# A spectral mixing layer and an expert layer in one kernel: neighbouring transfers of gathered token rows, of stage-2 blocks and of x joined into single ones

## The chip, the cores and the metric

The kernel runs as one launch on one core of a Trainium2 chip. The metric is device time in microseconds (us) of that core. TensorE (PE), VectorE (DVE), ScalarE (ACT), GpSimd (POOL) and SyncE (SP) run side by side, each through its own list of instructions in order. SP, ACT and POOL also issue transfers (DMAs), which sixteen DMA engines carry out.

## The reference, cut to what matters

```python
# x (8, 2496, 256); filters (1249, 256); float32
X = np.fft.rfft(x, axis=1)
y = np.fft.irfft(X * (filt_r + 1j * filt_i), n=2496, axis=1)

x = y.reshape(19968, 256)                 # the tokens
expert = token_ids * 2654435761 % 8
for e in range(8):                        # w1 (8, 256, 1024), w2 (8, 1024, 256)
    out[expert == e] = np.maximum(x[expert == e] @ w1[e], 0) @ w2[e]
```

Each of the eight batches is filtered along its 2496 positions by way of a Fourier transform, and then each token goes through the two matrices of the one expert that its id names.

## The kernel before, in words

**Mixing.** 2496 is split as 39 x 64. The position n is 64*n1 + n2, and the 64 values of n2 are laid out as three groups (h) of 21 with one left over. A batch passes through these steps:

- `load1` brings x in blocks (v = 0, 1, 2) of eight values of n2: partition 3*n1 + h of the block holds position 64*n1 + H0[h] + j, with H0 = (42, 0, 21). It issues one transfer per h, each of 39 partitions (line 249); the batch 0 one with h = 1 is issued by ACT, all others by SP.
- `stage1` multiplies by a DFT matrix of 39 (`wf`), and ACT stores the result to DRAM (`d1`, line 297, from 120 partitions).
- `load2` reads `d1` back turned, four frequencies at a time (`SG`): partition 2*n2 + p, where p says real or imaginary part. It issues one transfer per p on SP, each of 64 partitions (line 303).
- `forward` multiplies by a second DFT and by the filters, `back` goes the first step back, and ACT stores four frequencies at a time to `d2`, again one transfer per p (line 342).
- `load4` reads `d2` (SP, line 406), `stage3` takes the last step, and POOL scatters the finished tokens into `xs` in DRAM, sorted by expert (line 433).

Batches 0 and 1 keep part of this on the chip and do without `d2` or without both.

**Experts.** The sorted tokens lie in 85 tiles of 256 rows in `xs`; a row has 256 values and the token's number (`W` = 260 words). 80 tiles are always worked through (`NSURE`), five more if they are used. `load(i)` (line 835) fetches tile i: four transfers of 64 columns each into partitions 32*q to 32*q + 31 of the tile `xg`, and one transfer of the 256 token numbers into `no`. All are issued by ACT, but for those of tile 1 and the first three of tile 0, which SP issues. `token_parts` (line 852) turns `xg` by DVE into the operand of the products. `up` makes the first product, `down` the second; from tile 50 on (`WS`) `both` makes them. `store` scatters the rows to the output from POOL by the numbers in `no`.

**Order.** It is written out by hand: a list of (time in tiles, piece of work) pairs puts the mixing of batches 2 to 7 between the tiles. The tiles fall into five stages (they begin at tiles 0, 10, 20, 30 and 50); the first tile of a stage can be fetched only when the batches of that stage have been scattered. `ask` (line 1028) decides when a tile is fetched: inside `up` or `both`, just behind the ACT copy of the first product (lines 898 and 963) and ahead of ACT's relus (lines 891 and 953); or, within a stage, one tile sooner, inside `down`. `xg` has two buffers. Behind a tile's products SP issues the weights of the tile after next (lines 464, 467 and 469), 1 MB each.

Of the kernel before, what the change touches and what calls it, by code (L numbers as in the profile page):

```python
# [11 lines left out]
F32 = mybir.dt.float32  # L12
# [7 lines left out]
P = 128  # L20
B, S, C = 8, 2496, 256
# [7 lines left out]
N1, N2 = 39, 64  # L29
NS, NQ = N1 // 2 + 1, 64  # L30
H, HN = 3, 21
H0 = (2 * HN, 0, HN)
NR = H * N1
NK = 2 * H * NS
SG = 4
XG = 4
NU = (HN + XG) // XG
XL = 2 * XG
# [4 lines left out]
TB = 256  # L43
NT = (N + E * (TB - 1)) // TB
W = C + 4
# [28 lines left out]
def dft_tables():  # L74
    n1 = np.arange(N1)
    n2 = np.array([H0[i % H] + i // H for i in range(N2)])
    s, q = np.arange(NS), np.arange(NQ)
    ph = 2 * np.pi * np.outer(n1, s) / N1
    w = np.stack([np.cos(ph), -np.sin(ph)], 1)
    wf = np.zeros((N1, H, H, 2, NS))  # L80
    wi = np.zeros((H, 2, NS, H, N1))
    v = np.stack([2 * np.cos(ph), -2 * np.sin(ph)], 0)
    v[0, :, 0], v[1, :, 0] = 1.0, 0.0
    for h in range(H):
        wf[:, h, h] = w
        wi[h, :, :, h] = v.transpose(0, 2, 1) / S

    kap = np.where(q[:, None] < 32, s + N1 * q[:, None], s + N1 * (95 - q[:, None]))  # L90
    sg = np.where(q < 32, 1.0, -1.0)[:, None]
    th = 2 * np.pi * ((n2[:, None, None] * kap) % S) / S
    c, sn = np.cos(th), np.sin(th)
    d = np.zeros((2, N2, NS, 2, NQ))
    d[0, :, :, 0] = c.transpose(0, 2, 1)
    d[1, :, :, 0] = sn.transpose(0, 2, 1)
    d[0, :, :, 1] = (-sn * sg).transpose(0, 2, 1)
    d[1, :, :, 1] = (c * sg).transpose(0, 2, 1)
    f32 = np.float32
    return (wf.reshape(NR, NK).astype(f32), wi.reshape(NK, NR).astype(f32),  # L100
            d.transpose(1, 0, 2, 3, 4).reshape(P, NS, P).astype(f32))
# [24 lines left out]
def kernel(  # L126
# [9 lines left out]
):  # L136
    nc = tc.nc
    wf_host, wi_host, d_host = dft_tables()
    wf_dram = nc.inline_tensor(wf_host, name="wf_tbl")
    wi_dram = nc.inline_tensor(wi_host, name="wi_tbl")  # L140
# [42 lines left out]
    def slot(kind):  # L183
        slots[kind].append(slots[kind].pop(0))
        return slots[kind][-1]
# [30 lines left out]

    put_off = {2: [], 3: []}

    class Batch:


# [13 lines left out]
        def load1(self, v):  # L235

            k = self.b * NV + v if self.b < 2 else NV + NV * (self.b > 2) + v
            if self.b == 2 and v == 2:
                xt = x2pool.tile([NR, XL, C], F32, name="x_2_2", tag="x")
            elif k <= NV and self.b < 2:  # L240
                xt = wts[0:NR, k, :].rearrange("p (j c) -> p j c", c=C)
            else:
                xt = xpool.tile([NR, XL, C], F32, name=f"x_{self.b}_{v}", tag="x")
            self.x[v] = xt

            n = min(XL, HN + 1 - XL * v)
            for h in range(H):

                (nc.scalar if self.b == 0 and h == 1 else nc.sync).dma_start(out=xt[h:NR:H, 0:n, :],
                                  in_=bass.AP(tensor=x.tensor, offset=x.offset + (self.b * S + H0[h] + XL * v) * C,  # L250
                                              ap=[[N2 * C, N1], [C, n], [1, C]]))

        def products(self, w, rows, cols, src, dst, copy, u, name):

# [43 lines left out]

        def load2(self, g):
            t2 = slot("t2")  # L300
            for p in range(2):
                a0 = p * NS + SG * g
                nc.sync.dma_start(out=t2[p:P:2, :, :],
                                  in_=self.d1[:, a0:a0 + SG, :])
            self.t2[g] = t2

        def forward(self, u):
# [18 lines left out]
        def back(self, u):  # L326
            if self.d2 is None:
                self.d2 = dpool.tile([N2, 2 * NS, C], F32, name=f"d2_{self.b}", tag="d2")
            pr = self.p.pop(u)
            half = SG // 2  # L330
            if u % half == 0:
                self.g = slot("g")
            ps = fps.tile([P, 2, C], F32, name=f"pc_{self.b}_{u}", tag="f")
            for i in range(2):
                nc.tensor.matmul(out=ps[:, i, :], lhsT=e_t[:, 2 * u + i, :], rhs=pr[:, i, :],  # L335
                                 start=True, stop=True)
            i0 = 2 * (u % half)
            nc.scalar.copy(out=self.g[:, i0:i0 + 2, :], in_=ps[:])  # L338
            if u % half == half - 1:
                for p in range(2):  # L340
                    a0 = p * NS + SG * (u // half)
                    nc.scalar.dma_start(out=self.d2[:, a0:a0 + SG, :],
                                        in_=self.g[p:P:2, :, :])

        def stage1_c(self, u):
            v, j0 = divmod(XG * u, XL)
# [439 lines left out]
    head += [(98 + 5 * u, lambda u=u: second.stage3(u)) for u in range(NU)]  # L788
    head += [(99 + 5 * u - 3 * (u == 5), lambda u=u: third.stage1(u)) for u in range(NU)]
    head += [(123.5, lambda: begin()), (123.6, lambda: [load(i) for i in range(2)])]  # L790
    head += [(124, lambda: [nc.sync.dma_start(out=dram, in_=chip) for dram, chip in put_off[2]])]
    head += [(125 + .1 * g, lambda g=g: third.load2(g)) for g in range(4)]
# [23 lines left out]
    for e in range(E):  # L816
        t = 34.3 + 1.5 * e
# [8 lines left out]
    xg, to_rows, parts, rows = {}, {}, {}, {}  # L826
# [8 lines left out]
    def load(i):  # L835

        g = gath.tile([P, TB // 32, C // 4], F32, name=f"xg_{i}", tag="xg")
        no = nums.tile([P, 2], I32, name=f"no_{i}", tag="no")
        rows = xs[tiles[i] * TB:(tiles[i] + 1) * TB, :]
        moves = [(g[32 * q:32 * q + 32, :, :], rows[:, 64 * q:64 * q + 64].rearrange("(a t) c -> t a c", t=32))  # L840
                 for q in range(4)]
        moves.append((no[:].bitcast(F32), rows[:, C:C + 1].rearrange("(h p) c -> p (h c)", p=P)))
        for k, (to, src) in enumerate(moves):
            ld = (nc.sync if i < 2 and (i or k < 3) else nc.scalar).dma_start(out=to, in_=src)
            for b in range(STAGES[stage_of[i]], B):
                tc.declare_no_dep(ld.ins, group=f"xs_{b}", reason="the tiles of a stage hold tokens of its batches alone")
            if stage_of[i] < G - 1:
                tc.declare_no_dep(ld.ins, group="xs_pad", reason="places without a token lie in the last stage alone")
            tc.add_to_no_dep_group("xs_read", ld.ins)
        xg[i], to_rows[i] = g, no  # L850
# [177 lines left out]
    def ask(i, sooner=False):  # L1028

        j = asked[0]  # L1030
        if j <= i + 2 or (sooner and j == i + 3 < NT and stage_of[j] == stage_of[j - 1]):
            if j < NT:
                load(j)
                asked[0] += 1
# [48 lines left out]
    def rest(k):  # L1083
        with tc.If(used[0] > blocks[k][0]):
            for i in blocks[k]:
                ht = work.tile([P, 2, FP, P], F32, name=f"ht_{i}", tag="ht")
                if i >= NSURE + 2:
                    for j in ((i, i + 1) if i == NSURE + 2 else (i + 1,)):
                        if j < NT:
                            load(j)  # L1090
                    token_parts(i)
                token_sums(i)
                weight_sums(i, nc.vector)
                up(i, ht)
                weights(i + 2, 0)
                down(i, ht)
                store(i)
                weights(i + 2, 1)
            if k + 1 < len(blocks):
                rest(k + 1)  # L1100
# [30 lines left out]
```

## Time and profile before

| | us |
|---|---|
| median of 3 runs | 1428.36 (1425.63 to 1430.61) |
| the profiled execution | 1424.24 |
| its span in the trace | 1422.5 |

| engine | busy us | share of the span |
|---|---|---|
| PE | 1373.4 | 97% |
| DVE | 890.2 | 63% |
| POOL | 830.3 | 58% |
| ACT | 416.6 | 29% |

| transfers | issued by | count, KB each |
|---|---|---|
| `xg<-xs`, line 844 | ACT, SP | 321 and 7, 64 |
| `no<-xs`, line 844 | ACT, SP | 81 and 1, 1 |
| `mid<-d` (`load2`), line 303 | SP | 70, 256 |
| `d<-mid` (`back`), line 342 | ACT | 60, 256 |
| x (`load1`), line 249 | SP, ACT | 69 and 3, 312 or 234 |

In the profile, "waits" lists say which engine sat idle before which line and what ended it. A name with q (ACTq, SPq) is the engine's sequencer, which waits and issues transfers; while ACTq waits, ACT does nothing else. "DMA share" is the mean busy share of the sixteen DMA engines, by the durations of their packets. The span of 1422.5 us falls into a head of 122 us (batches 0 and 1, routing), a turn to the tiles (122 to 150), a middle in which tiles and mixing alternate (to 1043), and 370 us of tiles alone.

### The profile page before, as it was taken

To read this page: it belongs to the slowest core of one execution; us is meant where nothing else is said; L and a number is where in the kernel's file an instruction comes from. 1 tells how busy PE (TensorE), PEld (TensorE's weight loads), DVE (VectorE), ACT (ScalarE), POOL (GpSimd) and SP (SyncE) were. 2 spreads that over 40 slices of the span, in tenths; PEclk is the share of its full clock that TensorE was granted. 3 is DMA by queue.
4 is the path that set the end of the run, shared out by engine and by line. 5 is a ranking of instruction groups with operands and counts; after the bars stand their busy time and mean duration, and the time that the engine had idled before them with its cause. 6 is when DMAs were issued, how large, how long until landed. Compare 5 with 4: busy or idle time off the path is not lost.

```text
span 1422.5 us, 26307 instructions
## 1 busy us (share of the span) xinstructions
PE 1373.4 (97%) x9398; PEld 1273.3 (90%) x9398; DVE 890.2 (63%) x1636; ACT 416.6 (29%) x760; POOL 830.3 (58%) x736
## 2 busy tenths in 40 slices
PE   7898999999999999999999999999999999999997
PEld 7776888989888988889999899999999999999997
DVE  7773575575556566445665477657766776676775
ACT  4554122223232223232222222222222222222222
POOL 6167243844665565578533587788855566555563
PEclk9999899999999999999999999999999999999999
DMA  8677765757987698888755785887742526261611
GB/s 222 206 235 216 212 218 121 260 192 245 269 270 224 183 284 264 261 262 273 241 167 131 219 258 170 235 242 235 254 138 68 190 62 199 46 218 42 215 46 35
DMA packets 244505, 278.33 MB, mean 196 GB/s; under 512 B 125171, under 2 KB 213670, under 8 KB 234948
## 3 DMA queue, kind: packets, MB, share of 16 engines
q1 hardware_dynamic: 95149, 179.33, 40.2%
q10 hardware_dynamic: 129303, 52.69, 15.4%
q0 software_dynamic: 19920, 44.59, 8.9%
q8 instruction: 77, 1.26, 0.4%
q14 instruction: 56, 0.46, 0.1%
HBM read 293.65 MB, written 86.15 MB: 267 GB/s over the span
## 4 chain that ended last, share of the span: by engine, by line
PE 86%; DMA 8%; DVE 3%; issue 1%; ACT 1%; ACTq 0%; SPq 0%; POOLq 0%; POOL 0%; DVEq 0%
PE dps L922 22%; PE up_b L887 9%; PE up_a L887 6%; PE up_c L887 6%; PE pd L267 5%; PE pb L312 4%; PE dnc L949 4%; PE dnb L949 4%; PE dna L949 4%; PE upc L944 4%; PE upa L944 4%; PE pc L335 3%; PE pa L267 3%; DMA t<-d 2%; PE upe L944 2%; PE upb L944 2%
## 5 line engine op out<-in xcount | busy, mean ns | idle before, releaser
L922 PE MATMUL dps<-wts,ht 128*128 128x256 f32 x1600 | 370.9, 382 | 6.1 <-ACT ht L891 6.1
L922 PEld LDWEIGHTS dps<-wts,ht 128*128 128x128 f32 x1600 | 304.7, 192 | 50.6 <-ACT ht L891 7.3
L1014 POOL DMA_INDIRECT out_dram<-osb,no x158 | 165.2, 1046 | 219.2 <-DVE osb L956 137.8
L433 POOL DMA_INDIRECT xs<-o,sidx x176 | 177.0, 1006 | 168.7 <-ACT o L269 73.3
L877 POOL TENSOR_TENSOR tw<-wts 128x512 f32<-128x512 f32 x158 | 205.1, 1298 | 116.0 <-DMA wts<-in_moe_w_dram 92.4
L877 POOL TENSOR_TENSOR tw<-wts,tw 128x512 f32<-128x512 f32 x158 | 206.1, 1305 | 6.2
L894 DVE TENSOR_TENSOR ht<-up_b,ht 128x512 f32<-128x512 f32 x150 | 103.7, 691 | 114.6 <-PE up_b L887 91.2
L891 ACT ACTIVATE ht<-ht 128x512 f32<-128x512 f32 x150 | 94.3, 630 | 188.8 <-DVE ht L894 164.9
L322 DVE TENSOR_TENSOR z<-pb,filt 64x512 f32<-64x512 f32 x160 | 110.2, 689 | 30.9 <-PE pc L335 28.9
L927 DVE COPY osb<-dps 128x512 f32<-128x512 f32 x50 | 34.6, 691 | 150.2 <-PE dps L922 149.7
L887 PE MATMUL up_a<-xt,wts 128*128 128x128 f32 x800 | 115.3, 277 | 9.1 <-DVE xt L855 4.9
L887 PEld LDWEIGHTS up_a<-xt,wts 128*128 128x128 f32 x800 | 105.9, 193 | 12.7 <-DVE xt L855 5.3
L887 PE MATMUL up_b<-st,tw 128*128 128x128 f32 x800 | 107.4, 278 | 2.7 <-DVE ht L894 1.8
L887 PEld LDWEIGHTS up_b<-st,tw 128*128 128x128 f32 x800 | 98.1, 193 | 4.9 <-issue 3.7
L953 ACT ACTIVATE ht<-ht 128x512 f32<-128x512 f32 x90 | 56.6, 630 | 122.1 <-DVE ht L956 75.8
L894 DVE TENSOR_TENSOR ht<-up_c,ht 128x512 f32<-128x512 f32 x100 | 69.0, 690 | 37.2 <-PE up_c L887 32.4
L338 ACT COPY mid<-pc 128x512 f32<-128x512 f32 x60 | 35.0, 584 | 154.8 <-PE pc L335 91.5
L267 PE MATMUL pd<-t,wi_t 120*117 120x256 f32 x320 | 77.5, 385 | 2.6 <-DMA t<-d 2.6
L318 DVE TENSOR_TENSOR y<-pb,filt 128x512 f32<-128x512 f32 x80 | 55.1, 689 | 37.8 <-PE pb L312 35.6
L269 ACT COPY o<-pd 117x512 f32<-117x512 f32 x80 | 45.0, 585 | 104.4 <-DMA xg<-xs 45.4
L312 PE MATMUL pb<-mid,d_t 128*128 128x256 f32 x280 | 74.1, 388 | 1.1 <-DVE z L322 1.1
L898 ACT COPY ht<-up_a 128x512 f32<-128x512 f32 x50 | 29.3, 587 | 150.6 <-PE up_a L887 120.7
(210 smaller groups left out, 2466.1 us busy)
## 6 DMA issues: line engine op xcount, KB each, us to landing
wts<-in_moe_w_dram SPq DMA_DIRECT2D x162, 1024.0 KB
xg<-xs ACTq DMA_DIRECT2D x321, 64.0 KB
mid<-d SPq DMA_DIRECT2D x70, 256.0 KB
d<-mid ACTq DMA_DIRECT2D x60, 256.0 KB
d_t<-t2s SPq DMA_DIRECT2D x15, 1024.0 KB
e_t<-t2s SPq DMA_DIRECT2D x15, 1024.0 KB
x<-in_x_dram SPq DMA_DIRECT2D x39, 312.0 KB
t<-d SPq DMA_DIRECT2D x12, 960.0 KB
```

Source lines behind the costliest of these rows:

```text
L267: nc.tensor.matmul(out=ps[0:cols * H, k, :], lhsT=w[:], rhs=src[:, 2 * i + k, :], start=True, stop=True)
L312: nc.tensor.matmul(out=ps[:, i, :], lhsT=d_t[:, s, :], rhs=rhs, start=True, stop=True)
L322: nc.vector.tensor_tensor(out=z[b], in0=ps[a], in1=f_t[1][64 * hi:64 * hi + 64, s1:s1 + 2, :], op=OP.mult)
L433: st = nc.gpsimd.indirect_dma_start(out=xs[:], out_offset=bass.IndirectOffsetOnAxis(ap=index, axis=0), in_=rows, in_offset=None, bounds_ch ...
L877: eng.tensor_tensor(t[k][:], p, q, op=OP.subtract)
L887: nc.tensor.matmul(out=ps[bank][:, f, :], lhsT=w[:, f * P:(f + 1) * P], rhs=xx, start=first and f == 0, stop=True, skip_group_check=True)
L891: nc.scalar.activation(out=out, in_=in_, func=AF.Relu)
L894: nc.vector.tensor_tensor(out, ps[bank][:], other, op=OP.add)
L922: nc.tensor.matmul(out=ps[:, h, :], lhsT=ht[:, h, fp, :], rhs=w2[:, fp, :], start=(fp == 0), stop=(fp == FP - 1))
L944: nc.tensor.matmul(out=ps[:, f, :], lhsT=w[:, f * P:(f + 1) * P], rhs=xx, start=first and f == 0, stop=True, skip_group_check=True)
L949: nc.tensor.matmul(out=ps[:, 0, :], lhsT=a[:, f, :], rhs=b[:, f, :], start=first and f == 0, stop=True, skip_group_check=True)
L1014: st = nc.gpsimd.indirect_dma_start(out=out[:], out_offset=bass.IndirectOffsetOnAxis(ap=to_rows[i][:, h:h + 1], axis=0), in_=o[:, h, :], i ...
```

## The change

- `load1`: the three transfers of a block become one, of 117 partitions. Partition 3*n1 + h now holds position 64*n1 + 21*h + j; the rows of `wf` are put in that order on the host. Batch 0 has no x transfer on ACT any more.
- `load2` and `back`: the two parts p go in one transfer of 128 partitions; the DRAM side is read with (n2, p) as one index.
- `load`: the four transfers of a tile become one into all 128 partitions. Partition 32*q + t now holds the rows 8*t to 8*t + 7 of the tile, and the numbers in `no` are fetched in the order that fits. On the DRAM side the transfer has the dimensions (4 column blocks, 256 rows, 64 values), and that of the numbers (4, 64, 1) after merging; the chip side has 128 partitions in both. SP issues the rows of tiles 0 and 1 and the numbers of tile 1, ACT all else.

No arithmetic instruction is added or removed.

```diff
@@ dft_tables
-        wf[:, h, h] = w
+        wf[:, H0[h] // HN, h] = w
@@ class Batch
+    def halves(d):
+        return d[:].rearrange("n (p s) c -> (n p) s c", p=2)
@@ load1
-            for h in range(H):
-                (nc.scalar if self.b == 0 and h == 1 else nc.sync).dma_start(out=xt[h:NR:H, 0:n, :],
-                                  in_=bass.AP(tensor=x.tensor, offset=x.offset + (self.b * S + H0[h] + XL * v) * C,
-                                              ap=[[N2 * C, N1], [C, n], [1, C]]))
+            nc.sync.dma_start(out=xt[:, 0:n, :],
+                              in_=bass.AP(tensor=x.tensor, offset=x.offset + (self.b * S + XL * v) * C,
+                                          ap=[[N2 * C, N1], [HN * C, H], [1, n * C]]))
@@ load2
-            for p in range(2):
-                a0 = p * NS + SG * g
-                nc.sync.dma_start(out=t2[p:P:2, :, :],
-                                  in_=self.d1[:, a0:a0 + SG, :])
+            nc.sync.dma_start(out=t2, in_=halves(self.d1)[:, SG * g:SG * g + SG, :])
@@ back
-                for p in range(2):
-                    a0 = p * NS + SG * (u // half)
-                    nc.scalar.dma_start(out=self.d2[:, a0:a0 + SG, :],
-                                        in_=self.g[p:P:2, :, :])
+                g0 = SG * (u // half)
+                nc.scalar.dma_start(out=halves(self.d2)[:, g0:g0 + SG, :], in_=self.g)
@@ load
-        moves = [(g[32 * q:32 * q + 32, :, :], rows[:, 64 * q:64 * q + 64].rearrange("(a t) c -> t a c", t=32))
-                 for q in range(4)]
-        moves.append((no[:].bitcast(F32), rows[:, C:C + 1].rearrange("(h p) c -> p (h c)", p=P)))
+        moves = [(g[:], bass.AP(tensor=rows.tensor, offset=rows.offset, ap=[[C // 4, 4], [W, TB], [1, C // 4]])),
+                 (no[:].bitcast(F32), bass.AP(tensor=rows.tensor, offset=rows.offset + C, ap=[[W, 4], [8 * W, 32], [4 * W, 2], [1, 1]]))]
         for k, (to, src) in enumerate(moves):
-            ld = (nc.sync if i < 2 and (i or k < 3) else nc.scalar).dma_start(out=to, in_=src)
+            ld = (nc.sync if i < 2 and (i or k < 1) else nc.scalar).dma_start(out=to, in_=src)
```

## The prediction

> **What bounds the kernel now.** The page's busy table comes first (PE 97% of the span), then the chain of waits: 86% of it is PE and 8% is DMA. So PE sets the time wherever it has work, and a change to transfers can only win what PE idles, or make PE idle more. The PE records leave 40 us without work. The list of PE's waits shares out the gaps behind the head:
>
> ```profile
> PE dps L922 <- ACT ht L891: 6.1, 2, 3.1
> PE up_a L887 <- DVE xt L855: 4.9, 1, 4.9
> PE up_a L887 <- ACT ht L898: 4.2, 3, 2.0
> PE pd L267 <- DMA t<-d: 2.6, 2, 2.0
> ```
>
> Columns: total us, times, longest. The first and third lines, 10.3 us in five gaps (at 150, 396, 499, 605 and 789 us), are PE waiting for an ACT copy or relu. The timeline shows why ACT was late:
>
> ```profile
> 780.31 0.87 ACTq L297 DMA_DIRECT2D d<-mid  x2
> 781.27 3.20 ACTq L844 DMA_DIRECT2D xg<-xs  x4
> 790.32 0.38 ACTq L844 DMA_DIRECT2D no<-xs  x1
> 790.74 0.59 ACT L898 COPY ht<-up_a 128x512 f32<-128x512 f32 x1 [10.20 <-DMA xg<-xs]
> 791.38 0.71 PE L887 MATMUL up_a<-xt,wts 128*128 128x128 f32 x4 [1.98 <-ACT ht L898]
> ```
>
> ACT issues a tile's five transfers between its own pieces of work. In the records of the semaphores, the transfers of SP and ACT take eight completion semaphores in turn, and an issue waits until the transfer that held its semaphore before has landed. Here the `no` issue stood from 784.5 to 790.2 for the store of 780.31, the copy behind it was late, and PE lost 1.98 us.
>
> Second, how full the DMA engines are. By stretches (us; then busy us and count of each engine; PE clock, DMA share, GB/s):
>
> ```profile
> 250.00:350.00 100.00, 99.54 (x598) 90.05 (x597) 61.59 (x101) 30.12 (x54) 59.02 (x53) 1.00 0.74 235
> 350.00:450.00 100.00, 97.88 (x591) 88.29 (x590) 58.87 (x100) 30.68 (x55) 59.24 (x54) 1.00 0.87 260
> 450.00:550.00 100.00, 96.78 (x570) 86.61 (x570) 58.01 (x105) 26.97 (x49) 52.47 (x48) 0.98 0.82 245
> 550.00:650.00 100.00, 97.67 (x580) 86.76 (x580) 46.96 (x80) 30.30 (x55) 67.92 (x63) 1.00 0.84 259
> 1043.00:1200.00 157.00, 156.19 (x1394) 155.62 (x1393) 112.41 (x252) 43.50 (x89) 89.61 (x75) 1.00 0.42 127
> ```
>
> In the middle the sixteen engines are over 80% busy on average; in the last 370 us under half. What counts is therefore how evenly a joined transfer lies on them.
>
> **How a transfer is split.** The page's line for ACT's queue answers this:
>
> ```profile
> q10 hardware_dynamic: 129303, 52.69, 15.4%
> ```
>
> From the issues' counts and sizes, ACT's data packets are 82,176 of 256 B (321 `xg`), 20,736 of 4 B (81 `no`), 3,840 of 4 KB (60 `d<-mid`), 14,400 of 1 KB (other `d<-mid`) and 373 others: 121,525. That leaves 7,778 for completions. 490 transfers on sixteen engines each would give 7,840, 62 too many. Of the 490, three have 39 partitions, seventeen 120 and six 40: if each runs on the largest number up to 16 that divides its rows (13, 15, 10), 9 + 17 + 36 = 62 are missing. It fits exactly. So a transfer is split into equal numbers of outer rows. In every one of these both sides have the same number of rows. The new `xg` and `no` have 128 on the chip's side and 4 on the DRAM side; no row of before has such a pair. If the smaller decides, they run on 4 engines; if the chip's side does, on 16 as now. I take 4: a split in whole outer rows of a source with 4 of them has no more pieces.
>
> (The Trainium skill, "DMA: Bandwidth & Descriptors", section "Why a DMA increments its semaphore by 16 and not by 1", has the count of engines as the largest up to 16 that divides the slowest dimension of both sides; that is 4 here. The same page's "Rules for kernel authors" says to coalesce many small transfers into one large one. By the second rule alone the sum below would keep only its first term, about 1420; by the first it keeps all of them. The trace agrees with the first where the sides are equal, and shows no unequal pair.)
>
> **The change part by part.**
>
> x and stage 2: x goes from 72 transfers to 24; 39 and 117 rows both divide by 13, so the same 8 KB packets lie on the same 13 engines. `load2` goes from 70 to 35 and `back` from 60 to 30; 64 and 128 rows both give 16 engines and the same 4 KB packets. What goes are issues of 0.87, 0.63 and 0.57 us on SP and ACT, which PE covers (97.7 of 100 us busy in 550:650). In the head the chain is transfers of the same bytes. Cost 0; bounds -1 and 0.
>
> Issues on ACT: 893 transfers in all become 534, so a semaphore comes round later, and ACT issues two per tile instead of five (0.56 us each). The 10.3 us of gaps can go. What is late next is the tile's own data, so I take **-8**; bounds -10.3 and 0.
>
> The first tile: PE waits 4.9 us at 137 for tile 0. The chain has 2.31 us from the last of four issues (138.46) to landing. The joined one is issued at 137.6, once instead of in turns, but has 256 packets on each engine instead of 64. The trace's 256-byte packets take 20.6 ns on mean: 5.3 us instead of 1.3. First completions come 1.8 us after an issue here; landing about 137.6 + 1.8 + 5.3 = 144.7 instead of 140.8: **+3.5**; bounds -1 (sixteen engines) and +4.
>
> The middle: a tile's `xg` and `no` cost 1,024 x 20.6 + 256 x 9.1 ns = 23.4 us of engine time. That is 1.5 us on each of sixteen, but 5.9 on each of four: 4.4 more per tile on those four. 45 tiles are fetched in 250:1043, one in 17.6 us, so their share rises by 0.25: to 0.99, 1.12, 1.07 and 1.09 in the four stretches shown. Every other transfer that uses all engines ends when these four end. The part above 1 is 12 + 7 + 9 = 28 us. The shares hold waiting, though: 8 KB packets take 376 ns on mean, 309 at the fastest, 1 KB ones 58 and 46; at the fastest durations the shares are 17% lower and nothing is over 1. So 0 to 28; I take half, **+14**.
>
> Turns of a batch in the middle: the chain passes through transfers that end last there:
>
> ```profile
> 366.81 13.93 DMA t<-d
> 382.19 12.91 DMA wts<-in_moe_w_dram
> ...
> 586.18 5.45 DMA d<-mid
> 591.69 11.78 DMA t<-d
> ```
>
> Each stands behind up to one tile's rows more on the four engines, 4.4 us. There are five batches with a store and a load to and from `d2`; PE loses only 2.6 us at `t<-d` now, so most is covered by the tiles between. Of 5 x 4.4 = 22 I take **+6**; bounds 0 and 22.
>
> The last 370 us: ACT issues a tile's rows just behind the copy at line 963 and must then do its relus:
>
> ```profile
> 1101.53 2.28 ACTq L844 DMA_DIRECT2D xg<-xs  x4
> 1103.85 0.50 ACTq L844 DMA_DIRECT2D no<-xs  x1
> 1104.93 0.63 ACT L953 ACTIVATE ht<-ht 128x512 f32<-128x512 f32 x1 [2.82 <-DVE ht L956]
> ```
>
> The rows are needed one step (12.4 us) later by DVE. Alone they land in 1.8 + 5.9 us; beside 2 MB of weights on the same engines (64 packets of 1 KB and 8 of 8 KB at 46 and 309 ns: 5.4 us) in about 13. So only tiles with a change of expert on them lose something: **+3**; bounds 0 and 51 (rival 2).
>
> Sum: -8 + 3.5 + 14 + 6 + 3 = +18.5 on the profiled execution's 1424.2 gives 1442.7. That execution lies 4.1 us under the median of the runs, against which mine is compared: **1447 us**.
>
> **Rivals.**
>
> 1. *Sixteen engines after all.* Then only the first term is left, with -1 at the first tile: 1428.4 - 9 = about 1419, at best 1417. For it: the chip's side has 128 rows and could decide. Against: the exact divisors above. This is also the case in which the change does what its words say.
>
> 2. *ACT held behind its own long transfer.* When the queues are full, an `xg` issue takes up to 2.4 us instead of 0.46 (144.8 to 149.7, behind three stores: three in a row at 1.4 to 1.7), and PE then lost 3.1 us. If the `no` issue has to stand until the 256 packets ahead of it have gone out, ACT is held 0.4 + 5.3 + 0.5 = 6.2 us per tile instead of 2.8. In the last stretch the second product starts at 1106.7, 5.1 us after the first issue at 1101.5, and needs a relu of 0.63 us first: held over some 4.5 us, PE waits. 1.7 us x 30 tiles = 51 on top of the sum: 1447 + 51 = about 1498. It decides from 4.5 us held.
>
> 3. *Gain and load even out:* four engines, but the shares' waiting part gives way (terms of 0 to 4 us for the middle): 1428.4 - 8 + 3.5 + 4 = 1428.
>
> **How the numbers follow.** Forecast (four engines, +6 to +45 on the median) 0.42; rival 1 0.24; rival 2 0.2; rival 3 0.14. This kernel's measurement can tell 0.3%, 4.3 us. Rival 1 is faster but for a little, rival 3 mostly within: faster 0.25, within 0.3% 0.13, slower 0.62. The range goes from rival 1 (1416) to rival 2 (1498); the forecast's own range is 1434 to 1473.
>
> **What would show it.** On four engines the packets on ACT's queue are 121,152 of data and 1,471 completions, 122,623; on sixteen 124,555. PE's waits for ACT (lines 891 and 898 before) go from 10.3 to under 3 us. DVE's wait for the first `xg` grows by 3 us. The stretches 350 to 650 lengthen, with DMA shares no higher. In the last stretch ACT is held between the `xg` issue and its relu: under 4.5 us for the forecast, over it for rival 2. A shorter middle with PE at 98% would prove me wrong.

## The result, and the profile after

The changed kernel takes 1591.49 us in the median of six runs (1587.42 to 1595.99), the kernel before 1424.41 us in six beside it. The ratio is 1.118 (95% interval 1.115 to 1.122): 12% slower, far outside the predicted range. The profiled execution took 1590.27 us, with a span of 1588.6, 166.1 more than before.

From the page of the kernel after: PE's busy time, the line of ACT's queue, and the chain by engine.

```profile
PE 1418.0 (89%) x9398; PEld 1312.0 (83%) x9398; DVE 897.5 (56%) x1636; ACT 411.4 (26%) x760; POOL 825.4 (52%) x736
...
q10 hardware_dynamic: 122623, 51.72, 12.4%
...
PE 46%; ACTq 11%; DMA 2%; DVE 2%; ACT 1%; issue 1%; POOL 0%; POOLq 0%; DVEq 0%; SPq 0%
```

The 122,623 packets are those that four engines per tile fetch give, to the packet. The completions say it too: the semaphore of an `xg` transfer takes one step at once and then exactly four. New in the chain is ACTq, ACT's sequencer, with 11% (it was 0%).

PE's list of waits (total us, times, longest):

```profile
PE up_a L881 <- ACT ht L892: 56.0, 10, 15.3
PE dne L943 <- ACT ht L947: 43.9, 8, 7.9
PE dps L916 <- ACT ht L885: 21.4, 3, 15.5
PE up_a L881 <- DVE xt L849: 8.8, 1, 8.8
```

Lines 885, 892 and 947 are ACT's relus and copy (891, 898 and 953 before); `up_a`, `dps` and `dne` are products of `up`, `down` and `both`. The waits for these three lines were 10.3 us and are 121.3. The timeline at the longest issue of all (lines in between are left out):

```profile
389.47 0.55 ACTq L838 DMA_DIRECT2D xg<-xs  x1
390.14 22.15 ACTq L838 DMA_DIRECT2D no<-xs  x1
412.39 0.58 ACT L892 COPY ht<-up_a 128x512 f32<-128x512 f32 x1 [22.90 <-issue]
413.02 1.22 PE L881 MATMUL up_a<-xt,wts 128*128 128x128 f32 x4 [15.35 <-ACT ht L892]
```

The issue of `xg` is over in 0.55 us. The issue of the numbers behind it stands for 22.15 us; it is the duration of the issue itself that is long, not a wait for a semaphore ahead of it. The copy behind it is late, and PE idles 15.35 us. Over the whole run, this kind of issue takes 518 us of ACT (81 issues, median 4.36 us); it was 41 us before (0.46).

Where the time came from, by stretches that begin and end at the same work (the middle, then the tiles alone). Before, then after:

```profile
142.00:1044.00 902.00, 883.81 (x5394) 800.81 (x5395) 539.19 (x850) 246.47 (x438) 545.44 (x478) 0.99 0.75 228
1044.00:1415.00 371.00, 369.56 (x3300) 368.60 (x3298) 261.37 (x591) 102.41 (x206) 208.03 (x173) 1.00 0.38 111
```

```profile
142.00:1148.00 1006.00, 910.17 (x5396) 822.31 (x5396) 548.88 (x851) 244.04 (x438) 542.00 (x478) 0.95 0.66 205
1148.00:1581.00 433.00, 387.99 (x3296) 386.09 (x3296) 259.43 (x591) 99.44 (x206) 207.18 (x172) 0.94 0.31 94
```

The middle is 104 us longer and the last part 62. In the middle PE is without work for 96 us instead of 18, in the last part for 45 instead of 1. The rest is PE's own busy time, 26 and 18 us more for the same instructions, at a granted clock of 0.95 and 0.94 instead of 0.99 and 1.00. The DMA engines are less busy than before.

In the last part two kinds of tiles stand side by side. One without weights in flight, and one behind 2 MB of them (lines in between are left out here too):

```profile
1167.57 0.53 ACTq L838 DMA_DIRECT2D xg<-xs  x1
1168.14 3.18 ACTq L838 DMA_DIRECT2D no<-xs  x1
1171.37 1.15 ACT L947 ACTIVATE ht<-ht 128x512 f32<-128x512 f32 x2 [3.27 <-DVE ht L950]
...
1204.13 0.40 SPq L462 DMA_DIRECT2D wts<-in_moe_w_dram  x1
1204.88 0.33 SPq L464 DMA_DIRECT2D d_t<-t2s  x1
1205.09 0.53 ACTq L838 DMA_DIRECT2D xg<-xs  x1
1205.66 10.65 ACTq L838 DMA_DIRECT2D no<-xs  x1
1217.05 2.08 PE L943 MATMUL dne<-e_t,ht 128*128 128x128 f32 x8 [6.69 <-ACT ht L947]
```

Of the 29 issues in this part 21 take 2.7 to 3.7 us, and PE does not notice; eight take 8.1 to 11.6 us, and these are the eight waits of 43.9 us in all.

### The profile page after: what moved, and what is told of

Same layout as the page of the kernel before. It is cut to its first block, busy times and chain, and to the rows that moved or that the text cites. A ratio compares the mean times of both kernels' runs of the same rounds, so it can differ in the third digit from the quotient of the medians.

```text
span 1588.6 us, 25818 instructions
## 1 busy us (share of the span) xinstructions
PE 1418.0 (89%) x9398; PEld 1312.0 (83%) x9398; DVE 897.5 (56%) x1636; ACT 411.4 (26%) x760; POOL 825.4 (52%) x736
## 3 DMA queue, kind: packets, MB, share of 16 engines
q10 hardware_dynamic: 122623, 51.72, 12.4%
## 4 chain that ended last, share of the span: by engine, by line
PE 46%; ACTq 11%; DMA 2%; DVE 2%; ACT 1%; issue 1%; POOL 0%; POOLq 0%; DVEq 0%; SPq 0%
ACTq L838 10%; PE dps L916 8%; PE up_b L881 5%; PE dnc L943 4%; PE dna L943 4%; PE dnb L943 3%; PE up_a L881 3%; PE up_c L881 3%; PE upa L938 3%; PE upc L938 2%; PE dne L943 2%; PE pc L334 1%; PE pd L269 1%; PE upe L938 1%; PE upb L938 1%; PE upg L938 1%
## 5 line engine op out<-in xcount | busy, mean ns | idle before, releaser
L881 PE MATMUL up_a<-xt,wts 128*128 128x128 f32 x800 | 123.6, 290 | 64.8 <-ACT ht L892 56.0
L881 PEld LDWEIGHTS up_a<-xt,wts 128*128 128x128 f32 x800 | 113.0, 204 | 70.2 <-ACT ht L892 58.3
L881 PE MATMUL up_b<-st,tw 128*128 128x128 f32 x800 | 114.2, 289 | 1.9 <-DVE ht L888 1.4
L881 PEld LDWEIGHTS up_b<-st,tw 128*128 128x128 f32 x800 | 104.8, 204 | 3.7 <-issue 3.4
L199 DVE TENSOR_TENSOR filt<-ht 128x512 f32<-128x512 f32 x60 | 42.3, 705 | 73.7 <-ACT ht L947 73.7
```

The lines of the kernel that those rows point to most:

```text
L881: nc.tensor.matmul(out=ps[bank][:, f, :], lhsT=w[:, f * P:(f + 1) * P], rhs=xx, start=first and f == 0, stop=True, skip_group_check=True)
```

## The experiments

Each kernel ran beside runs of the kernel before on the same chip; the chips differ (the kernel before takes 1453 us on those of the first eight, 1428 us on that of the last two), so ratios to it are given. The expected times in us were written for a chip like that of the first runs. Where an edit changes the list of transfers, the index in the line of the issuing engine is set to fit, so that ACT and SP issue the same parts as in the change. Theory A, formed from the profile after: the numbers' issue holds ACT until the 256 packets per engine ahead of it have been handed out. Theory B: four engines are too full, and all that uses them is late. Theory C: the joined x and stage 2 have a share in it.

**Everything but the fetch** (the four transfers and the numbers as before):

```diff
-        moves = [(g[:], bass.AP(..., ap=[[C // 4, 4], [W, TB], [1, C // 4]])), ...]
+        moves = [(g[32 * q:32 * q + 32, :, :], rows[:, 64 * q:64 * q + 64].rearrange("(a t) c -> t a c", t=32))
+                 for q in range(4)]
+        moves.append((no[:].bitcast(F32), rows[:, C:C + 1].rearrange("(h p) c -> p (h c)", p=P)))
```

> The joined x and stage-2 transfers stay; a tile is fetched in four transfers and its numbers in a fifth, as before. Theory A (ACT is held by the issue of the numbers behind a 256 KB transfer that lies on four engines) and theory B (those four engines are full, and everything that shares them is late) both put the whole loss into the tile's fetch: 1412 to 1426 us. Theory C (part of the loss comes from the joined x or stage-2 transfers): over 1440 us.

Measured: 0.998 (0.9957 to 1.0004), 1451.3 us. By ratio that is 1421 us on the first chip: no loss, and no gain that can be told.

**The fetch alone** (the converse edit on the kernel before):

```diff
-        moves = [(g[32 * q:32 * q + 32, :, :], ...) for q in range(4)]
+        moves = [(g[:], bass.AP(..., ap=[[C // 4, 4], [W, TB], [1, C // 4]])), ...]
```

> Only the tile's fetch is joined; x and stage 2 as before. A and B: 1580 to 1605 us, like the whole change. C: clearly less, under 1560 us.

Measured: 1.114 (1.109 to 1.118), 1620.1 us. By ratio (1586 us on the first chip) it is the whole loss. C is out.

**The numbers ahead of the rows:**

```diff
-        moves = [(g[:], ...), (no[:].bitcast(F32), ...)]
+        moves = [(no[:].bitcast(F32), ...), (g[:], ...)]
```

> The whole change, but the token numbers are issued ahead of the tile's rows, so nothing of the same fetch stands behind the long transfer. The same packets lie on the same four engines. A: ACT is released after some 1 us per tile unless another of its stores follows soon, and most of the loss goes: 1430 to 1480 us. B: the four engines are as full as before, 1570 to 1600 us.

Measured: 1.030 (1.025 to 1.035), 1495.6 us. The order of two issues alone gives back three quarters of the loss, with the same packets on the same engines. A foretold that (1467 us on the first chip); B did not. The median issue of the numbers is 0.53 us. Most of what is left comes from the next issue behind the long transfer, wherever it falls: PE still waits 32.7 us for line 892, and in this run's trace a tile's rows issued at 385.2 us land at 426, and the next tile's numbers, issued at 399.6, stand for 17.8 us.

**One transfer, sixteen engines:**

```diff
-        moves = [(g[:], bass.AP(..., ap=[[C // 4, 4], [W, TB], [1, C // 4]])), ...]
+        moves = [(g[:], bass.AP(..., ap=[[2 * W, P], [C // 4 + 1, 8], [1, C // 4]])),
+                 (no[:].bitcast(F32), rows[:, C:C + 1].rearrange("(h p) c -> p (h c)", p=P))]
```

> The whole change, with one 256 KB transfer of 1,024 packets of 256 bytes per tile, but with a DRAM side whose outer dimension is 1,024, so that it runs on sixteen engines; the token numbers are fetched as before, also on sixteen. The columns of the tile are then not in their places, so the rows of the output are other numbers, with the same work. A and B: no loss is left, 1412 to 1424 us. If it is the length of one transfer that holds ACT and not the number of its engines: about 1590 us.

Measured: 0.985 (0.981 to 0.988), 1429.0 us (1403 on the first chip, a little better than either theory had it). With the same joins on sixteen engines the change is a gain of 1.5%; the loss is in the number of engines. As x and stage 2 alone give 0.998, most of the gain is in the joined fetch; no run has that fetch without the other joins.

**Four transfers, each on four engines:**

```diff
-                 (..., rows[:, 64 * q:64 * q + 64].rearrange("(a t) c -> t a c", t=32))
+                 (..., bass.AP(..., offset=rows.offset + 64 * q, ap=[[W, 4], [4 * W, TB // 4], [1, C // 4]]))
```

> x and stage 2 joined as in the change, and a tile's rows again in four transfers of 64 columns, but with a DRAM side whose outer dimension is 4, so that each of the four runs on four engines; the numbers on sixteen, as before. The rows stand in another order than their numbers, so the rows of the output are exchanged within a tile; the work is the same. Theory A in its sharper form (ACT is held because 256 packets per engine must take their turns on four engines): ratio to before 1.08 to 1.13. If joining four transfers into one is what costs: 0.99 to 1.01.

Measured: 1.109 (1.102 to 1.116), 1609.2 us. With as many transfers as before, the loss is there again.

**One transfer on eight engines:**

```diff
-        moves = [(g[:], bass.AP(..., ap=[[2 * W, P], [C // 4 + 1, 8], [1, C // 4]])),
+        moves = [(g[:], bass.AP(..., ap=[[C // 4 + 1, 8], [2 * W, P], [1, C // 4]])),
```

> As the run with one transfer per tile on sixteen engines, but the DRAM side has an outer dimension of 8, so that the same 1,024 packets of 256 bytes lie on eight engines, 128 on each; the columns are not in their places, so the output is other numbers with the same work. If the packets per engine set how long ACT is held, it lies between sixteen engines (0.985) and four (1.118): 1.00 to 1.05, and the shortest issue of the numbers behind it between 0.66 and 3.06 us, near 1.5 us.

Measured: 1.027 (1.024 to 1.031), 1491.6 us. The lines of the numbers' issue (ns: shortest, median, longest) with sixteen, eight and four engines; in the second and third the shortest is tile 0's, with nothing ahead of it:

```profile
L838 ACTq DMA_DIRECT2D no<-xs x81: 366/671/8027, 145.9 to 1406.5; - x81
```

```profile
L838 ACTq DMA_DIRECT2D no<-xs x81: 407/2092/12681, 144.8 to 1471.0; - x81
```

```profile
L838 ACTq DMA_DIRECT2D no<-xs x81: 627/4361/22152, 135.6 to 1569.1; - x81
```

The fastest tenth takes up to 0.66, 1.19 and 3.06 us for 64, 128 and 256 packets per engine: the issue is longer the more packets are ahead. I had expected 1.5 us for the middle one. The packet records show until when it stands. When the issue of the numbers ends, about 100 packets of the rows per engine have still to start, taken as evenly spread: 99 in the median of the kernel after, 98 of 128 here. With sixteen engines all 64 have still to start, and the median issue takes 0.67 us. So theory A is right but for its end: in the median ACT stands until some 155 of the 256 have gone, not all.

**The whole change, issued by SP:**

```diff
-            ld = (nc.sync if i < 2 and (i or k < 1) else nc.scalar).dma_start(out=to, in_=src)
+            ld = (nc.sync if i or k < 1 else nc.scalar).dma_start(out=to, in_=src)
```

> The whole change with both transfers of a tile issued by SP. The same packets lie on the same four engines, but it is SP that is held. Theory A (the loss is ACT held while its copies and relus are due): 1.00 to 1.05 of before, since SP runs ahead of its consumers by a step or more. Theory B (the four engines are late for all): 1.09 to 1.13.

Measured: 1.007 (1.004 to 1.009), 1463.2 us. Its numbers' issue:

```profile
L838 SPq DMA_DIRECT2D no<-xs x81: 2887/5622/15419, 143.2 to 1434.6; - x81
```

It stands as long as on ACT (511 us in all, for 518), on the same four engines and again until about 100 packets are left (median 101), but now it is SP that stands there. Two of PE's waits in this run:

```profile
PE pd L269 <- DMA t<-d: 8.5, 3, 4.8
PE up_a L881 <- ACT ht L892: 3.0, 1, 3.0
```

The waits for ACT's lines 885, 892 and 947, 121.3 us in the change, are the 3.0 us of the second line. Sixteen seventeenths of the loss are gone (0.118 to 0.007) by the choice of the issuing engine alone: by far the most of it was ACT, held while its copies and relus were due. The 0.7% is not the price of the four engines as such. The next run, on the same chip, fetches from SP on sixteen engines and takes 24 us less (1.7%). That is the four engines, SP's standing and the joined fetch together; no run parts them.

**A version that beats both:** x and stage 2 joined, the fetch in five transfers on sixteen engines, issued by SP:

```diff
-            ld = (nc.sync if i < 2 and (i or k < 3) else nc.scalar).dma_start(out=to, in_=src)
+            ld = (nc.sync if i or k < 3 else nc.scalar).dma_start(out=to, in_=src)
```

> x and stage 2 joined, the tile fetched in five transfers on sixteen engines as before, but all issued by SP (the numbers of tile 0 alone by ACT). If ACT's time for issues is what PE lost before (10.3 us of waits for ACT copies and relus): 0.98 to 0.995 of before. If SP, held by semaphores and by the scattered rows, brings the weights late instead: 1.00 to 1.03.

Measured: 0.991 (0.988 to 0.994), 1439.2 us. To see which half gains, the same edit on the kernel before, and this one again beside it:

> The kernel before with one edit: all five transfers of a tile are issued by SP (the numbers of tile 0 alone by ACT). If ACT's time for the issues is the whole gain of the run with the joined x and stage 2 and the fetch on SP: the same 0.985 to 0.995. If SP, with 72 + 70 separate issues of its own and the same eight semaphores, gets too full without the joined ones: 0.995 to 1.02.

> The same kernel as the run with x and stage 2 joined and the fetch on SP, on the chip and beside the runs of the one without the joins: 0.985 to 0.996 again.

Measured: 1.008 (1.005 to 1.010), 1436.1 us, without the joins; 0.989 (0.986 to 0.993), 1412.1 us, with them. Moving the five transfers to SP pays where x and stage 2 have been joined, and costs 0.8% where they have not; so ACT's time for issues is not the whole gain. Joining x and stage 2 gives nothing that can be told while ACT issues five transfers per tile (0.998). Fewer rounds of the eight semaphores may be the reason; no run shows it by itself.

## Why the prediction was wrong, point by point

- *How a transfer is split:* right, to the packet (122,623). The Trainium skill ("DMA: Bandwidth & Descriptors", "Why a DMA increments its semaphore by 16 and not by 1") had the divisor of both sides; the runs agree for a pair of 128 and 4, with four completions.
- *x and stage 2 cost nothing:* right while ACT issues the fetch in five transfers (0.998).
- *"ACT issues two per tile instead of five (0.56 us each). The 10.3 us of gaps can go":* the step that failed. It took an issue's price from issues behind transfers that put 16 packets on an engine. Behind one that puts 256 there, the second issue took 6.4 us on mean, ACT's two 7.0 in all, and the gaps went to 121.3 us. The term was -8 and is +111 of idle PE.
- *First tile +3.5:* PE's gap went from 4.9 to 8.8 us, +3.9, but the agreement is partly luck. The rows were issued at 135.6 us, not 137.6, and landed 6.1 us later, for 7.1 worked out; PE came to the wait 3.2 us sooner, and its first product starts only 0.75 us later than before (142.60 for 141.85).
- *Middle, +14 for four engines over their capacity:* right in sign, wrong in mechanism for by far the most. With the same packets on the same engines, issued by SP, PE is busy for 293 of the 300 us from 350 to 650, at DMA shares of 0.82, 0.74 and 0.90. The middle was 104 us longer because ACT stood: 51 issues of the numbers took 376 us there.
- *Turns of a batch, +6:* not seen. PE's wait for `t<-d` is 1.8 us in the kernel after, for 2.6 before. It is 8.5 us with the fetch from SP on four engines, but 6.8, 7.1 and 10.4 us in the three runs with the fetch from SP on sixteen, so it goes with SP as the issuer and not with the four engines.
- *Last part, +3:* it is +62, 44 of idle PE and 18 of PE's longer busy time. Rival 2 had the mechanism, and its point of 4.5 us held fits: issues of up to 3.7 us cost PE nothing, all eight over 8 cost it 5.5 us each on mean. But it spread one price, 1.7 us, over 30 tiles where 21 paid nothing and eight three times as much. It had all 256 packets go out first, where 155 do, and it did not count the weights' packets between them: during each of the eight issues SP's transfers move 2 to 3 MB, during the other 21 nothing. And it priced nothing in the middle, where the engines are twice as busy. So it got 0.2 and 1498 us instead of the first place and some 1590.
- *No term for the clock:* 45 of the 166 us are PE's longer busy time for the same instructions, at a granted clock of 0.948 instead of 0.990.

The row that should have weighed more was in the prediction: `xg` issues of 1.4 to 1.7 us at 144.8 us, when the queues were full, and PE's 3.1 us behind them. (The last 1.8 us there, 149.7 to 151.5, are a wait for a semaphore.) It showed that an issue itself can be long; it was used for a rival's price in one part only.

## What to carry to other kernels

Before joining transfers, look at the outer dimension of both sides: what counts is packets per engine, and one transfer of four outer rows is a queue of 256 on four engines. Ask which engine issues the next transfer behind it, and what work that engine owes; the order of two issues was worth 9%, and the choice of the issuing engine 11%. A long queue belongs on an engine with little due, here SP; a short one, on sixteen engines, was better still.

## What the runs showed of the hardware

- An issue is not always cheap. That of the numbers took 0.46 us in the median with short queues, and up to 22 us behind a queue of 256 packets on its engines, with the issuing engine idle all the while. In the median it ended when about 100 of them were left.
- Such a queue drains slowly where others are busy. The 256-byte packets take 18.3 ns each on mean, 4.7 us for 256. During the 22.15 us of the longest issue 718 of the 1,024 start, 180 on each of the four engines, and these from 394.4 us on: one per 100 ns. The stretch of that issue in the kernel after, with the columns as above:

```profile
390.00:412.00 22.00, 7.68 (x48) 6.89 (x46) 1.75 (x8) 0.00 (x0) 10.85 (x10) 0.72 1.01 300
```

All sixteen engines were busy then (share 1.01), most of all with SP's packets of 1, 4 and 8 KB. From 394.4 us to the end of the issue 2,861 of these start, 179 on each of sixteen engines if they lie evenly: as many as of the small ones. That is no rule of one for one. In the four issues of 9.6 to 11.6 us in the last part, beside weights mostly in packets of 8 KB, 141 to 161 of the small ones start on each of the four engines and only 12 to 15 of SP's. The Trainium skill says that an engine goes round its queues packet by packet ("DMA: Bandwidth & Descriptors", "Queues, rings and completion order"), and that such a packet typically holds 9 to 17 descriptors. No run here shows these turns: the records have starts and sizes, but not how many go in one turn.
- PE's granted clock was lower where PE idled more: 0.990 with 40 us idle, 0.970 with 92 (numbers first), 0.948 with 162, 0.942 with 175 (four on four). In the line above it is 0.72. If the idle time is the reason, it cost over a third more than itself, 45 us on 121; no run changes the one without the other.
